# Hash attention and a gated MLP: a third Strassen product of the gated layer computed by halves, with its weight factors made in the first chunk

## The chip, the cores and the metric

The kernel runs on one core of a Trainium2 chip. The metric is device time in microseconds (us); the kernel before took 866.93 us (median of 3 runs, 865.80 to 868.44). TensorE (PE in the profile) multiplies, VectorE (DVE) and ScalarE (ACT) work on tiles, GpSimd (POOL) and SyncE (SP) mostly issue DMAs here. PEld is TensorE's loading of weights, which the profile lists beside the matmuls.

## The reference

```python
# attention: B=4, H=8, S=768, D=64; proj is [64, 6]
q_bits = (einsum('bhsd,dk->bhsk', q, proj) > 0)        # k_bits alike
mask   = q_bucket[:, :, :, None] == k_bucket[:, :, None, :]   # the 6 bits as a number
attn   = softmax(where(mask, q @ k.T / sqrt(D), -1e9))
x = (attn @ v).transpose(0, 2, 1, 3).reshape(3072, 512)
# the MLP: w_in [512, 2048], w_out [2048, 512]
r = maximum(x @ w_in, 0)
return (r * r) @ w_out                                   # float32, [3072, 512]
```

## The kernel before, in words

**Stages.** The attention comes first (0 to 317 us of the span; L341 to L812). It leaves x, transposed, in DRAM. The MLP then goes over the tokens in three chunks of 1024: a *gated layer* (x times w_in, then relu squared) followed by `project` (times w_out). The order of all work is written out by hand, so on every engine and every DMA queue the instructions run in the order of the program. A DMA that GpSimd, SyncE or ScalarE issues waits in that engine's own queue.

**The gated layer.** A chunk's h is 2048 x 1024: sixteen blocks of 128 rows, taken as eight *units* r, each of two row blocks (r and r + 8) times two halves of 512 tokens. Each unit is one level of Strassen-Winograd: seven products in place of eight, named by their token-side factor: "11", "21", "t1", "t2", "t3", "t4", "22". A product has two matmuls (f = 0, 1) of 128x128 weights and 512 columns. The weight-side factors of all units lie in DRAM as `w_in_7`; `load_unit` (L641) brings one unit's to SBUF on SyncE's queue. Sums go to banks acc0, acc1, acc2 of PSUM; partial sums that are used more than once are copied out by ScalarE: `one`, `two`, `three`, `five` (L842 in chunk 0, L1062 later; two buffers each). VectorE adds the copies to banks, and gates: h·max(h, 0), one instruction (L919). The gated results are b11, b12, b21, b22, from which sums for the next layer are made at once (b_t, b12 in the loop at L1338 and below; `inner_sums` L1099).

**Chunks 1 and 2 of the gated layer** go by four *pairs* of units, n and n + 4 (`hidden_pair` L1046). Of two of the seven products ("21" and "t4") both units' work is put together as one product of 512 columns and four row blocks, and this is done by a second level of Strassen-Winograd: seven matmuls of 256 columns in place of eight (that is, of four of 512). That is `inner_steps` (L995): four steps of two, two, two and one matmul, and `put` (L1039), which adds the inner result to the outer sums and gates it. Its matmuls are at L1007; its partial sums are copied into quarters of two `o` tiles (`snaps`). The first inner product runs in a pair's first half, the second in its second half, step by step between the outer products (L1054). The inner weight factors are sums over both units' weights. `factor_units` (L956) makes them for pair n during chunk 0's projection, in its products k = 1 to 4: GpSimd loads two `h` tiles of `w_in_7`, VectorE sums, GpSimd stores to `w_in_49` (L969). `load_inner` (L971) brings them back, on SyncE's queue, one pair ahead; for a chunk's first pair at product k = 6 of the chunk before. The token-side factors are `sums_inner` (L985), made in the hook of k = 6.

**`project`** (L1176) is one level over seven outer products k, each of which is again `product` (L826), by 256 columns. Each takes leaf tiles of w_out (128 x 512), asked for on ScalarE's queue (L1121). Its sums go to `sum0` to `sum3`, `tmp` and `o` (L1131), and out.

**Other things beside.** A guard decides whether a second, general program has to run: `load_peak` (L868) has GpSimd load q and k in 32 pieces of 128 x 2 x 384 (`raw_qk`, two buffers), and `peak` (L874) reduces each to its largest magnitudes, two in every unit of chunks 1 and 2, on VectorE, at the end of the unit. The guard's test is not met by this input in either kernel. In chunk 0 the factors of w_out are made too (`sums_out`, L1291, and `sums_out_49`, in units 0 to 5); after unit 5 their pool `p_1` is closed, and the pool `p_y` with leaf, sum, t, o and tmp tiles is opened. The x of the next chunk (2 MB) is asked for on GpSimd's queue at k = 0 of `project` (L633).

Of the kernel before, what the change touches and what calls it, by code (L numbers as in the profile page):

```python
# [27 lines left out]
PLAIN = 30.0  # L28
# [6 lines left out]
def kernel(  # L35
# [49 lines left out]
    w_in_49 = p_d.tile([NQ, P, 2, 7, P], FP32, name="w_in_49")  # L85
# [556 lines left out]
    def load_unit(n, pool=p_i):  # L642

        if n < NCHUNK * NR and n not in w_unit:
            r = order(n)
            w_unit[n] = pool.tile([P, 7, NFT // 2, P], FP32, name="w_unit", bufs=2 if pool is p_i else 1)
            m = 7 if n < NR else 5
            nc.sync.dma_start(out=w_unit[n][:, 0:m], in_=w_in_7[r, :, 0:m])
# [8 lines left out]
    with tc.manual_schedule():  # L657
# [167 lines left out]

        def product(n, w, at, bt, c11, c12, c21, c22, hook=None):  # L826

            acc = [ps_m.tile([P, 512], FP32, name=f"acc{i}")[:, 0:w] for i in range(3)]

            def add(to, a, b, first, last):
                for i in range(n):
                    nc.tensor.matmul(  # L835
                        out=acc[to], lhsT=a(i), rhs=b(i), start=first and i == 0,
                        stop=last and i == n - 1, skip_group_check=True,
                    )

            def keep(of, name):  # L840
                t = p_r.tile([P, 512], FP32, name=name)[:, 0:w]
                nc.scalar.copy(out=t, in_=acc[of])  # L842
                return t

            add(0, at(0), bt["11"], True, False)
            one = keep(0, "one")
            add(1, at(1), bt["21"], True, True)
            if hook:
                hook()
            c11(acc[1], one)  # L850
            add(0, at(4), bt["t2"], False, False)
            two = keep(0, "two")
            add(2, at(3), bt["t1"], True, False)
            five = keep(2, "five")
            add(0, at(5), bt["t3"], False, False)
            three = keep(0, "three")
            add(2, at(6), bt["22"], False, True)
            c12(acc[2], two)
            c22(three, five)
            add(0, at(2), bt["t4"], False, True)  # L860
            c21(acc[0])
# [12 lines left out]
        def peak(i):  # L874

            nc.vector.tensor_reduce(  # L876
                out=peaks[:, :, i], in_=raw_qk.pop(i), axis=AXL.X, op=ALU.max,
                apply_absolute_value=True,
            )
# [9 lines left out]
        def guard():  # L889

            most = p_k.tile([1, 2], FP32, name="most")
            tp = spare("tp")[:, 0]
            for w in range(2):
                nc.tensor.transpose(
                    out=tp[0:1, w * P:(w + 1) * P], in_=top[:, w:w + 1], identity=ident
                )
            nc.vector.tensor_reduce(
                out=most, in_=tp[0:1, 0:2 * P].rearrange("o (w f) -> o w f", w=2), axis=AXL.X,
                op=ALU.max,
            )  # L900
            nc.vector.tensor_scalar(
                out=slow, in0=most[:, 0:1], scalar1=most[:, 1:2], scalar2=PLAIN / (scale * D),
                op0=ALU.mult, op1=ALU.is_gt,
            )
# [26 lines left out]
        def hidden(i, r):  # L931
# [4 lines left out]
            def gate(out):  # L936
# [11 lines left out]
                gate(b22),  # L948
# [5 lines left out]
        w_inner, t_inner, snaps, now = {}, {}, {}, {}  # L954

        def factor_units(n):  # L956
# [9 lines left out]
            for lo, hi, t in (  # L966
                (0, 2, src[0]), (2, 3, src[1][:, :, 1:2]), (3, 5, sums[0]), (5, 7, sums[1])
            ):
                nc.gpsimd.dma_start(out=w_in_49[n, :, :, lo:hi], in_=t)  # L969

        def load_inner(i, n):  # L971

            if n < NQ:
                w_inner[i, n] = []
                for j, name in enumerate((("sum0", "sum3"), ("sum2", "sum1"))[n % 2]):
                    t = p_y.tile([P, 4, QN], FP32, name=name).rearrange("p a (b c) -> p (a b) c", c=P)
                    nc.sync.dma_start(out=t[:, 0:7], in_=w_in_49[n, :, j])
                    w_inner[i, n].append(t)

        def quarters_x(i, j):  # L980

            b = xs[i][0][:, 2:4, 0:HN] if j == 0 else xs[i][0][:, 0:2, HN:NCH]
            return b[:, 0, 0:QN], b[:, 0, QN:HN], b[:, 1, 0:QN], b[:, 1, QN:HN]

        def sums_inner(i):  # L985

            t_inner[i] = [p_y.tile([P, NQ, QN], FP32, name=f"t{m}", bufs=2) for m in range(2)]
# [7 lines left out]
        def inner_steps(i, n, j):  # L995
# [5 lines left out]
            if i not in snaps:  # L1001
                o = [p_y.tile([P, HN], FP32, name="o", bufs=NOUT) for _ in range(2)]
                snaps[i] = [o[m // 2][:, m % 2 * QN:(m % 2 + 1) * QN] for m in range(4)]
            one, two, three, five = snaps[i]

            def mul(out, a, b, start, stop):
                nc.tensor.matmul(  # L1007
                    out=out, lhsT=w[:, a], rhs=b, start=start, stop=stop, skip_group_check=True
                )

            def step_0():
                a0, a1 = (ps_m.tile([P, 512], FP32, name="acc1")[:, 0:QN] for _ in range(2))
# [7 lines left out]
            def step_1():  # L1020
                hs["a2"] = spare("acc3")[:, 0, 0:QN]
# [24 lines left out]
        def hidden_pair(i, n, half):  # L1046

            r = half * NQ + n
            w, bt = w_unit.pop(i * NR + 2 * n + half), factors_x(i)
            acc = {m: ps_m.tile([P, 512], FP32, name=f"acc{m}") for m in (0, 2)}  # L1050

            def add(to, a, b, first, last):
                for f in range(NFT // 2):
                    nc.tensor.matmul(  # L1054
                        out=acc[to], lhsT=w[:, PLACE[a], f], rhs=bt[b](f),
# [4 lines left out]
            def keep(of, name):  # L1060
                t = p_r.tile([P, 512], FP32, name=name)
                nc.scalar.copy(out=t, in_=acc[of])  # L1062
                return t

            if half == 0:
                load_inner(i, n + 1)
                now[0], now[1] = (inner_steps(i, n, j) for j in range(2))
            *steps, put = now[half]
            add(0, 0, "11", True, False)
            one = keep(0, "one")  # L1070
            if half:
                now[0][4](1, b11[:, r], one)
            else:
                steps[0]()
            add(2, 3, "t1", True, False)
            five = keep(2, "five")
            steps[1 - half]()
            add(0, 4, "t2", False, False)
            two = keep(0, "two")
            steps[2 - half]()  # L1080
            if half == 0:
                put(0, b11[:, r], one)
            add(2, 6, "22", False, True)
            gate_sum(b12[:, r], acc[2], two)
            steps[3 - half]()
            if half:
                put(0, b21[:, n], now["three"])
            add(0, 5, "t3", False, True)
            three = keep(0, "three")
            gate_sum(b22[:, r], three, five)  # L1090
            if half:
                steps[3]()
                put(1, b21[:, r], three)
            now["three"] = three
# [82 lines left out]
        def project(i):  # L1177
# [60 lines left out]
            for k in range(7):  # L1238
# [6 lines left out]
                if k == 6 and more:  # L1245
                    load_inner(i + 1, 0)
# [8 lines left out]
                def hook():  # L1255
# [4 lines left out]
                    if k == 6 and more:  # L1260
                        sums_inner(i + 1)
# [73 lines left out]
        for i in range(NCHUNK):  # L1335
            for s in range(NR):
                r = order(i * NR + s)
                if i == 0:  # L1338
                    hidden(i, r)
                else:  # L1340
                    hidden_pair(i, s // 2, s % 2)
                minus(b_t[:, r], b12[:, r], b11[:, r])
# [7 lines left out]
                if i == 0 and r == THEN[-1]:  # L1350
                    p_1s.close()
                    p_y = fast.enter_context(tc.tile_pool(name="p_y", bufs=1, reuse_waits="tile"))
                load_unit(i * NR + s + (3 if i == 0 and s < 2 else 2))
# [5 lines left out]
                if i > 0 and s % 2:  # L1359
                    inner_sums(0, slice(s // 2, s // 2 + 1))  # L1360
                minus(b12[:, r], b22[:, r], b12[:, r])
                for n in range(2):
                    m = 2 * ((i - 1) * NR + s) + n
                    if m >= 0:
                        peak(m)
# [241 lines left out]
```

## Time and profile before

| | us |
|---|---|
| median of 3 runs | 866.93 |
| the profiled execution, own time | 866.47 |
| its span, first to last instruction | 864.2 |
| mean granted clock of TensorE | 0.998 of full |

Stages of the span, from the busy times of each engine in the stretches (the bounds are rounded; DMA is the mean busy share of the 16 DMA engines):

| stage | us | PE busy | PEld | DVE | ACT | POOL | DMA |
|---|---|---|---|---|---|---|---|
| attention | 0–317 | 314.3 | 149.8 | 292.3 | 240.8 | 67.5 | 0.81 |
| chunk 0, gated layer | 317–413 | 96.0 | 42.6 | 82.5 | 24.2 | 35.6 | 0.85 |
| chunk 0, project | 413–499 | 84.8 | 74.0 | 77.5 | 11.8 | 21.5 | 0.85 |
| chunk 1, gated layer | 499–592 | 93.0 | 51.8 | 74.7 | 30.4 | 14.9 | 0.52 |
| chunk 1, project | 592–677 | 85.0 | 74.6 | 76.7 | 12.0 | 8.0 | 0.71 |
| chunk 2, gated layer | 677–770 | 93.0 | 51.8 | 73.7 | 30.8 | 14.9 | 0.48 |
| chunk 2, project | 770–855 | 84.9 | 74.0 | 69.9 | 11.6 | 5.2 | 0.59 |
| last output | 855–864 | 0.8 | 0.4 | 1.4 | 0.4 | 1.3 | 0.34 |

A row is read like this: in chunk 1's gated layer TensorE is busy all of the 93 us, VectorE 80% of them, and the transfers half. In the lists of groups a line such as `PE MATMUL acc<-t_x,w_unit 128*128 128x512 f32 x192` names engine, operation, the tile written, the tiles read, the weights' and the output's shapes, and the count. What follows in brackets is idle time and the instruction that ended it. A float32 matmul leaves two records. In the timeline, the first number is the start and the second the duration, in us.

### The profile page before, as it was taken

Reading aid. Unit: us, or ns where it says so; the run is one execution under the profiler, and the core shown is the slowest. Engines: PE = TensorE matmul, PEld = TensorE weight load, DVE = VectorE, ACT = ScalarE, POOL = GpSimd, SP = SyncE. Lnnn points to the kernel's source line nnn. Section 1 sums busy time; section 2 is a strip of 40 time slices with the busy share of each in tenths; the row PEclk is TensorE's granted clock in tenths of the full one; section 3 lists DMA queues with packets and bytes.
Section 4 is the critical chain, followed back from the end, with each engine's and each line's share of the span. In section 5 each row is a group of like instructions: output and inputs, shape, how many; then the busy total and the mean of one; then the engine's idle time right before and its main releaser. Section 6 shows DMA issues by size and latency. Waiting matters only on the chain.

```text
span 864.2 us, 16743 instructions
## 1 busy us (share of the span) xinstructions
PE 851.8 (99%) x6548; PEld 519.2 (60%) x6548; DVE 748.8 (87%) x1005; ACT 362.0 (42%) x648; POOL 168.9 (20%) x284
## 2 busy tenths in 40 slices
PE   8999999999999999999999999999999999999996
PEld 3544444444444444444888855557888655568885
DVE  5899999999999898988879978888799688888875
ACT  5887777888777752222111133332111233321110
POOL 1321111123221102642132211112001111100002
PEclk9999999999999999999999999999999999999999
DMA  9677799879997618999888864547757645355565
GB/s 206 129 152 148 178 182 205 203 166 257 244 229 192 200 53 276 317 322 284 292 269 258 177 168 157 176 120 263 246 156 191 161 157 175 118 162 159 147 185 98
DMA packets 226629, 168.03 MB, mean 194 GB/s; under 512 B 167112, under 2 KB 184848, under 8 KB 226544
## 3 DMA queue, kind: packets, MB, share of 16 engines
q1 hardware_dynamic: 187744, 87.19, 40.7%
q0 software_dynamic: 16416, 41.95, 15.7%
q10 hardware_dynamic: 22384, 37.76, 14.6%
q8 instruction: 53, 0.87, 0.4%
q14 instruction: 32, 0.26, 0.1%
HBM read 124.52 MB, written 41.68 MB: 192 GB/s over the span
## 4 chain that ended last, share of the span: by engine, by line
PE 98%; DVE 1%; issue 0%; POOL 0%; ACT 0%; POOLq 0%; DVEq 0%
PE acc L835 40%; PE st L430 18%; PE acc L1054 16%; PE xo L485 14%; PE acc L1007 6%; PE tot L534 2%; PE hash L360 1%; PE xo L337 1%; PE tp L320 0%; DVE bits L410 0%; DVE o L1131 0%; POOL out_dram L1152 0%; PE xo L360 0%; ACT e L436 0%; DVE tmp L1131 0%
## 5 line engine op out<-in xcount | busy, mean ns | idle before, releaser
L436 ACT ACTIVATE e<-st 128x768 f32<-128x768 f32 x192 | 155.3, 809 | 58.6 <-PE st L430 55.5
L430 PE MATMUL st<-feat 64*64 64x384 f32 x1536 | 157.4, 483 | 1.0 <-DVE feat L329 1.0
L485 PE MATMUL xo<-e,v_nat 64*64 64x385 f32 (+1 forms) x1520 | 157.1, 483 | 0.0
L835 PE MATMUL acc<-b,leaf 128*128 128x256 f32 x600 | 133.2, 379 | 1.2 <-issue 1.2
L835 PEld LDWEIGHTS acc<-b,leaf 128*128 128x128 f32 x600 | 113.8, 190 | 17.7 <-issue 2.3
L473 DVE TENSOR_TENSOR total<-total,e 128x1536 f32<-128x1536 f32 x64 | 111.7, 1746 | 4.3 <-ACT e L436 2.8
L396 POOL DMA_DIRECT2D bits<-signed x120 | 61.9, 520 | 218.2 <-ACT signed L385 199.6
L485 PEld LDWEIGHTS xo<-e,v_nat 64*64 64x64 f32 (+1 forms) x1520 | 56.3, 133 | 67.5 <-issue 59.3
L1054 PE MATMUL acc<-t_x,w_unit 128*128 128x512 f32 x192 | 90.2, 592 | 0.0
L430 PEld LDWEIGHTS st<-feat 64*64 64x64 f32 x1536 | 55.9, 133 | 39.3 <-issue 33.9
L835 PE MATMUL acc<-t,leaf 128*128 128x256 f32 x336 | 76.2, 380 | 0.0
L835 PEld LDWEIGHTS acc<-t,leaf 128*128 128x128 f32 x336 | 63.7, 190 | 9.1 <-DVE t L593 0.5
L919 DVE SCALAR_TENSOR_TENSOR b<-h 128x512 f32<-128x512 f32 x96 | 65.7, 691 | 3.0
L430 PE MATMUL st<-bits 64*64 64x384 bf16 x768 | 65.0, 325 | 0.1
L1054 PE MATMUL acc<-x,w_unit 128*128 128x512 f32 x128 | 60.2, 592 | 0.0
L835 PE MATMUL acc<-x,w_unit 128*128 128x512 f32 x128 | 56.5, 593 | 0.0
L1054 PEld LDWEIGHTS acc<-t_x,w_unit 128*128 128x128 f32 x192 | 36.5, 190 | 28.9 <-issue 26.8
L835 PE MATMUL acc<-b_t,leaf 128*128 128x256 f32 x240 | 53.8, 379 | 0.0
L1152 POOL DMA_DIRECT2D out_dram<-h x26 | 16.8, 654 | 174.1 <-DVE h L1145 167.0
L842 ACT COPY two<-acc 128x256 f32<-128x256 f32 (+1 forms) x29 | 12.5, 431 | 87.8 <-PE acc L835 75.3
L835 PEld LDWEIGHTS acc<-b_t,leaf 128*128 128x128 f32 x240 | 45.5, 190 | 6.2
L872 POOL DMA_DIRECT2D raw_qk<-in_q_dram x32 | 17.3, 541 | 162.4 <-DVE peaks L876 162.4
(155 smaller groups left out, 1194.2 us busy)
## 6 DMA issues: line engine op xcount, KB each, us to landing
leaf<-w_out ACTq DMA_DIRECT2D x142, 256.0 KB, 3.1
w_unit<-w_in SPq DMA_DIRECT2D x16, 640.0 KB, 4.0
raw<-in_moe_w_in_dram SPq DMA_DIRECT2D x8, 1024.0 KB, 6.3
raw<-in_moe_w_out_dram SPq DMA_DIRECT2D x8, 1024.0 KB, 7.4
w_unit<-w_in SPq DMA_DIRECT2D x8, 896.0 KB, 9.2
w_out<-sums POOLq DMA_DIRECT2D x16, 448.0 KB, 8.0
sum<-w_in SPq DMA_DIRECT2D x16, 448.0 KB, 4.9
v_nat<-in_v_dram SPq DMA_DIRECT2D x16, 384.0 KB, 5.1
```

The lines of the kernel that those rows point to most:

```text
L396: nc.gpsimd.dma_start(out=t[h * D:h * D + NBITS + 1, w, c * HS:(c + 1) * HS], in_=signed[at:at + NBITS + 1, h],)
L430: nc.tensor.matmul(out=st[k * HK:(k + 1) * HK, h, 0:HS], lhsT=src[1][rows, key], rhs=src[0][rows, cut], start=first, stop=not first, skip_ ...
L436: nc.scalar.activation(out=key_of(pr, kt)[:, :, i, 0:HS], in_=st[:, :, 0:HS], func=ACTF.Exp, scale=scale)
L473: nc.vector.tensor_tensor(out=totals[pr], in0=totals[pr], in1=e, op=ALU.add)
L485: return nc.tensor.matmul(out=outs[pr][h * D:(h + 1) * D, c, 0:HS + 1], lhsT=nat[pr, "v_nat"][rows, h, kt * D:(kt + 1) * D], rhs=key_of(pr ...
L534: done = nc.tensor.matmul(out=spares[pr][g * 32:(g + 1) * 32, c2, 0:QS], lhsT=ones[rows], rhs=totals[pr][rows, h, c, c2 * QS:(c2 + 1) * QS ...
L835: nc.tensor.matmul(out=acc[to], lhsT=a(i), rhs=b(i), start=first and i == 0, stop=last and i == n - 1, skip_group_check=True,)
L872: nc.gpsimd.dma_start(out=raw_qk[i][:, w], in_=flat[:, i * n:(i + 1) * n])
L919: nc.vector.scalar_tensor_tensor(out=out, in0=h, scalar=0.0, in1=h, op0=ALU.max, op1=ALU.mult)
L1007: nc.tensor.matmul(out=out, lhsT=w[:, a], rhs=b, start=start, stop=stop, skip_group_check=True)
L1054: nc.tensor.matmul(out=acc[to], lhsT=w[:, PLACE[a], f], rhs=bt[b](f), start=first and f == 0, stop=last and f == NFT // 2 - 1, skip_group_ ...
L1152: queue.dma_start(out=out[at, m0 + a * 32:m0 + (a + 1) * 32].rearrange("(c i) j -> i c j", i=32), in_=ot[a * 32:(a + 1) * 32].rearrange("i ...
```

## The change

Three things change, and some orders with them.

- **A third product by halves.** In chunks 1 and 2 the product "22" of both units of a pair also becomes an inner product of seven 256-column matmuls. The three are now called A ("21"), B ("22") and C ("t4"). `hidden_pair` is put in a new order: A's steps and B's first two in the first half, B's last two and C's in the second. "22" no longer shares acc2 with "t1"; instead VectorE adds `five` to `two` (tiles of 128x512), and B's `put` adds that sum to the inner result for b12. As the sums of b_t, b12 and of the next layer need b12 of both units, they move into the second half.
- **Its weight factors** are not made in `factor_units`, but for all four pairs at once in chunk 0: after unit 5, GpSimd loads the "22" weights of all units (two loads of 512 KB, into `sum0` and `sum1`); VectorE sums them in the hook of the last unit (four instructions), and GpSimd stores them (four DMAs) as a third plane of `w_in_49`. They come back in two leaf tiles a pair (`load_third_inner`), on SyncE's queue at the pair's first half for the next pair, and for a chunk's first pair on ScalarE's queue in the hook of k = 6. `load_unit` brings four factors in place of five (512 KB for 640). `sums_inner` makes a third set of four sums.
- **The first inner weights** of a chunk are asked for in two parts, at k = 5 and at k = 6, where both were asked for at k = 6.
- **The peaks** become squares with a running sum on ScalarE, four in a unit of 384 elements each, spread over the half; the guard's limit is squared to match.
- **Buffers.** `two` and `five` have one buffer in place of two, while `one` and `three` keep two. Inner copies use two sets, which alternate.

The diff, cut to its core:

```diff
-    w_in_49 = p_d.tile([NQ, P, 2, 7, P], FP32, name="w_in_49")
+    w_in_49 = p_d.tile([NQ, P, 3, 7, P], FP32, name="w_in_49")
...
-            m = 7 if n < NR else 5
+            m = 7 if n < NR else 4
...
+        KEPT = dict(one=2, two=1, three=2, five=1)
...
-                t = p_r.tile([P, 512], FP32, name=name)[:, 0:w]
+                t = p_r.tile([P, 512], FP32, name=name, bufs=KEPT[name])[:, 0:w]
...
-            nc.vector.tensor_reduce(
-                out=peaks[:, :, i], in_=raw_qk.pop(i), axis=AXL.X, op=ALU.max,
-                apply_absolute_value=True,
+            t = raw_qk[i][:, w]
+            nc.scalar.activation(
+                out=t, in_=t, func=ACTF.Square, accum_out=peaks[:, w, i:i + 1]
             )
...
+        def load_thirds():
+            for j in range(2):
+                thirds[j] = p_y.tile([P, 4, QN], FP32, name=f"sum{j}").rearrange(
+                    "p n (f c) -> p n f c", c=P
+                )
+                nc.gpsimd.dma_start(
+                    out=thirds[j],
+                    in_=w_in_7[j * NQ:(j + 1) * NQ, :, PLACE[6]].rearrange("n p f c -> p n f c"),
+                )
+        def sum_thirds():
...
+            sums_a(
+                *(thirds[j][:, :, f] for j in range(2) for f in range(2)),
+                *(sums[m // 2][:, :, m % 2] for m in range(4)),
+            )
+            for lo, hi, t in (
+                (0, 2, thirds[0]), (2, 3, thirds[1][:, :, 1:2]), (3, 5, sums[0]), (5, 7, sums[1])
+            ):
+                nc.gpsimd.dma_start(
+                    out=w_in_49[:, :, 2, lo:hi].rearrange("n p m c -> p n m c"), in_=t
+                )
...
+        def load_third_inner(i, n, queue):
+            if n < NQ:
+                ts = [p_y.tile([P, NQ, P], FP32, name="leaf", bufs=NLEAF) for _ in range(2)]
+                for m, t in enumerate(ts):
+                    hi = min(4 * m + 4, 7)
+                    queue.dma_start(out=t[:, 0:hi - 4 * m], in_=w_in_49[n, :, 2, 4 * m:hi])
+                w_inner[i, n].append(lambda a: ts[a // 4][:, a % 4])
...
-                snaps[i] = [o[m // 2][:, m % 2 * QN:(m % 2 + 1) * QN] for m in range(4)]
-            one, two, three, five = snaps[i]
+                o = [o[m // 2][:, m % 2 * QN:(m % 2 + 1) * QN] for m in range(3)]
+                snaps[i] = o, [t_inner[i][m][:, 3] for m in range(3)], spare("acc3")
+            side = (3 * n + (0, 2, 1)[j]) % 2
+            one, two, five = snaps[i][side]
+            three = one
+            last = snaps[i][2][:, side, 0:QN]
...
-                a0, a1 = (ps_m.tile([P, 512], FP32, name="acc1")[:, 0:QN] for _ in range(2))
+                a0, a1 = (ps_m.tile([P, 512], FP32, name=f"acc{m}")[:, 0:QN] for m in (1, 2))
...
+            A, B, C = (now[c] for c in "ABC")
+            add(acc, 0, "11", True, False)
+            one = keep(acc, "one")
             if half == 0:
+                A[0]()
             else:
+                B[2]()
+                C[0]()
+                A[4](1, b11[:, r], one)
+                B[4](0, b12[:, r0], now["two"])
+            mark()
+            other = ps_m.tile([P, 512], FP32, name="acc2")
+            add(other, 3, "t1", True, True)
+            five = keep(other, "five")
             if half == 0:
+                A[1]()
+            else:
+                B[3]()
+                C[1]()
+                minus(b_t[:, r0], b12[:, r0], b11[:, r0])
+                minus(b12[:, r0], b22[:, r0], b12[:, r0])
+            mark()
             add(acc, 4, "t2", False, False)
+            two = keep(acc, "two")
             if half == 0:
+                A[2]()
+                B[0]()
+                A[4](0, b11[:, r], one)
+                nc.vector.tensor_tensor(out=two, in0=two, in1=five, op=ALU.add)
+            else:
+                C[2]()
+                nc.vector.tensor_tensor(out=two, in0=two, in1=five, op=ALU.add)
+                B[4](1, b12[:, r], two)
+                minus(b_t[:, r], b12[:, r], b11[:, r])
+                inner_sums(0, slice(n, n + 1))
+                C[4](0, b21[:, r0], now["three"])
+            mark()
             add(acc, 5, "t3", False, True)
+            three = keep(acc, "three")
             if half == 0:
+                A[3]()
+                B[1]()
+                gate_sum(b22[:, r], three, five)
             else:
+                C[3]()
+                gate_sum(b22[:, r], three, five)
+                minus(b12[:, r], b22[:, r], b12[:, r])
+                C[4](1, b21[:, r], three)
+            mark()
...
-                if k == 6 and more:
-                    load_inner(i + 1, 0)
+                if k >= 5 and more:
+                    load_inner(i + 1, 0, (k - 5,))
...
+                        load_third_inner(i + 1, 0, nc.scalar)
...
-                    hidden(i, r)
+                    hidden(i, r, sum_thirds if s == NR - 1 else None)
...
+                    load_thirds()
...
-                    if m >= 0:
-                        peak(m)
```

## The prediction

> **What bounds the kernel now.** I read the summary first, then the chain of work that ended last, then who waited for whom on TensorE, then the timeline of one pair of units engine by engine.
>
> ```profile
> PE 851.8 (99%) x6548; PEld 519.2 (60%) x6548; DVE 748.8 (87%) x1005; ACT 362.0 (42%) x648; POOL 168.9 (20%) x284
> ...
> PE 98%; DVE 1%; issue 0%; POOL 0%; ACT 0%; POOLq 0%; DVEq 0%
> ```
>
> TensorE (PE) is the bound: 98% of the chain is its own work. On TensorE's list of waits all four together are 4.5 us, none of them in a pair. So a matmul column removed is time removed, as long as no new wait opens. The price of a matmul is the distance of groups in the chain (start, length, records; a float32 matmul is two records):
>
> ```profile
> 499.52 1.72 PE acc L1054 x4
> 501.24 0.86 PE acc L1007 x4
> 502.10 1.72 PE acc L1054 x4
> ```
>
> Two matmuls of 512 columns take 1.72 us, so 0.859 each; two of 256 take 0.86, so 0.430 each, with no loss for alternating. A pair now is 2x10x0.859 + 14x0.430 = 23.2 us; the chain has pairs starting at 522.73 and 545.94, 23.2 apart.
>
> **TensorE work removed.** Each pair trades four 512-column matmuls ("22", two f in two units) for seven of 256: 4x0.859 - 7x0.430 = 0.43 us. Four pairs in each of two chunks: 8x0.43 = **3.44 us** less. The pair becomes 16x0.859 + 21x0.430 = 22.8 us: first half 4 products (6.87) and eleven 256s (4.73), 11.6; second half 6.87 and ten 256s, 11.2.
>
> **A new short gap.** In the second half the copy `two` of acc0 must end before product "t3" adds to acc0, and only C's third step, two 256-column matmuls or 0.86 us, lies between. Before, at least 1.72 us lay there. Three rows of before price it; the first two are one pair's step and copy, the third a load that waited:
>
> ```profile
> 529.45 1.03 PE L1007 MATMUL acc<-x,sum 128*128 128x256 f32 x4
> ```
>
> ```profile
> 529.64 0.58 ACT L1062 COPY two<-acc 128x512 f32<-128x512 f32 x1 [1.34 <-PE acc L1054]
> ```
>
> ```profile
> 855.76 0.53 PEld L1162 LDWEIGHTS acc<-ident,o 128*128 128x128 f32 x4 [1.23 <-DVE o L1131]
> ```
>
> The copy starts 0.20 after the next group's first matmul and lasts 0.585 (group mean). That VectorE `o` started at 855.63 and took 0.41, so a waiting weight load starts 0.05 after its releaser: here at 0.84. The load itself waits, it doesn't go ahead. The first matmul of the first unit also began with its load not yet done: its record is 0.697 against 0.592, so an uncovered load costs 0.105. Thus "t3" starts at 0.84 + 0.105 = 0.945 where 0.859 was free: 0.086 us a pair, 8x = **0.69 us**. Bounds: nothing, if the load may go ahead (0.84 is under 0.859); 0.84 + 0.19 (whole load) - 0.859 = 0.17, or 1.37 in all. I take the row of a load that waited. TensorE's page of the Trainium skill ("TensorE: Matmul & The Clock Gate", section "Architectural detail: the array is 16× 32×32, not 1× 128×128") says that the queue can pull weight loads ahead of running matmuls; by it the term would be nothing, rival 1. The trace's only clear case, at 855.76, has the load waiting with its matmul.
>
> **VectorE (DVE).** Removed: 32 peaks of 0.945, four a pair. Added per pair: three 256-column adds of the new inner product (0.42 each) and two sums two+five (0.69 each). The total falls by 1.1 us a pair; what matters is the order, because the second half now holds most of it. The timeline's spacing is 0.60 for a 512-column instruction, 0.72 if the next needs its result; 0.34 and 0.45 at 256. Second half, TensorE's start as 0: C's third step is through at 9.03, seen by VectorE at 9.23. Behind it stand two adds 0.68, two+five 0.72, the b12 gate 1.44, b_t 0.60, three inner sums 1.13, the b21 gate 1.32, the b22 gate 1.44, b12 0.60, the last b21 gate 1.32: 9.25. VectorE ends at 18.5, TensorE at 11.2: **7.3 us late**. Before it was as late, through the peaks: the next half began at 522.57, and
>
> ```profile
> 528.14 1.81 DVE L876 TENSOR_REDUCE peaks<-raw_qk 128x2 f32<-128x768 f32 x2
> 529.87 0.41 DVE L1017 TENSOR_TENSOR h<-acc,o 128x256 f32<-128x256 f32 x1
> ```
>
> What is queued behind: the next pair's first add frees an acc2 bank at 7.3 + 0.41 + 0.05 = 7.76. B's first step wants that bank at 1.72+0.86+1.72+0.86+1.72+0.86+0.43 = 8.17, less 0.105 for the load: 8.06. Covered by 0.3; I take nothing. It decides from a lag of 7.6 on (rival 2). The single `five` buffer is freed by the b22 gate at 15.2 - 11.2 + 0.7 = 4.7 where its copy could start at 4.5; the copies then have 1 us of cover.
>
> **ScalarE (ACT).** Gains five copies of about 0.375 and eight squares a pair. A 384-element square with a running sum isn't in the trace; nearest, the 32x384 sign at L371 is 0.571 and the 384-element copy at L327 0.478; above, the 770-element copy 0.797. I take 0.57; the ends differ by 0.3, and ScalarE works some 14.9 of 22.8 us. The square ahead of the critical `two` can end 1.3 us before that copy is due, so both ends cost nothing. "ScalarE: Activation LUTs" in the Trainium skill (section "What ACT_TABLE_LOAD costs") gives 186 ns + 0.833 per element, an estimated 0.51; the sum would be the same. A square also waits for its raw_qk: GpSimd asks once the tile is read, two issues of 0.54 and 3.3 to landing, 4.4 in all where about 8 us lie between.
>
> **First chunk.** GpSimd's queue gets two loads of 512 KB and four stores, ahead of the peak loads, x and the `h` loads. The loads take the place of four raw_qk issued at 398.0 to 400.2, landing 6 us later; I put them at 406. VectorE's four sums (2.5) then end at 408.5, the gate behind (1.3) at 409.8; VectorE stood idle 5.01 us there until 411.81. Nothing lost. At the slowest GpSimd load's 12.5 us they land at 411.7: the first outer product's sums come 3.8 late, cover 1.4, so 2.4 us lost. The x load waits for TensorE until 414.23 anyway, and the first `h` land at 428.2 to 429.4 for a use at 432.85.
>
> The 1.25 us gap at 460 in the chain, called issue, ends when VectorE's b<-b,t (459.98, 1.22) does; VectorE had waited 5.20 us for an `h` load at 443.45. The change leaves that order: I keep it, bounds -1.25 to +1.25.
>
> **Other moves.** sums_inner is four adds longer (1.6 us): at the second entry VectorE freed the last acc2 at 676.1, then 677.7, wanted at 679.6. Asking for inner weights a product sooner, the smaller unit loads (512 for 640 KB) and 448 KB more per pair: no matmul waited for a DMA, and DMA share is 0.48 to 0.52 there; nothing, either way.
>
> **Sum.** The profiled execution took 866.47 us (span 864.2 and 2.3 around it): 866.47 - 3.44 + 0.69 = **863.7**. It is 0.46 under the median of the runs shown; from 866.93 it would be 864.2. About 0.3%, 2.6 us, is what a measurement of this kernel can tell from no change, and the forecast (-0.32%) lies just past it.
>
> **Rivals.**
> 1. The weight load goes ahead, no gap at "t3": 866.47 - 3.44 = 863.0. For: 0.84 against 0.859. Against: 855.76.
> 2. Slower: VectorE's backlog at the pair's seam holds the acc2 bank. Place: B's first step of the six pairs that follow a pair; price six times what the lag is over 7.6. If VectorE's 17 instructions took their full record and 0.05 each (9.66 + 0.85 for 9.25), the lag is 8.56 and the loss 5.8: 869.5. For: a cover of only 0.3. Against: before's spacing is shorter than its records, and the same lag is measured.
> 3. The thirds land late, or the gap at 460 grows: +1.3 to +2.4, about 865.5. For: the DMA engines are full from 380 to 405 (0.82 to 1.01 by windows). Against: the idle 5.01.
>
> **How the numbers follow.** Forecast 0.53, of which 0.39 past the bound and 0.14 short of it; rival 1 0.16; rival 2 0.15, of which 0.12 over 869 and 0.03 between; rival 3 0.16, of which 0.01 slower. Faster 0.39 + 0.16 = 0.55; slower 0.13; within 0.32. The forecast's own range is 862.9 to 864.8. With the lower end of the gap at 460 and rival 3, the range is 862.2 to 867.0: rival 2 and a little on either side are left out.
>
> **What would show it.** TensorE's records 48 more, busy near 848.4; pairs 22.8 to 22.9 apart. `two` ends 0.79 after C's third step begins, and "t3" begins 0.95 after it (0.86: rival 1). The first add of a pair starts 7.3 after the pair (over 7.6, with B's second matmul late: rival 2). Square near 0.57. The first chunk's sums start by 407, the first outer product unbroken. A wait on ScalarE for raw_qk, or on TensorE for VectorE in a pair, would make the forecast wrong.

## The result, and the profile after

The changed kernel takes **864.43 us** (median of 18 runs, 863.23 to 866.64); the kernel before took 866.76 (median of 18 runs, 865.54 to 869.26). The ratio is 0.9973, with a 95% interval of 0.9964 to 0.9982: 2.3 us less, 0.27%. The forecast from the median was 864.2; the profiled execution took 863.55 us (span 861.4) where 863.7 was forecast.

The page of the changed kernel (busy time, share of the span, instructions), and from it the engines' shares of the chain that ended last:

```profile
PE 849.1 (99%) x6596; PEld 529.3 (61%) x6596; DVE 748.9 (87%) x1025; ACT 408.2 (47%) x816; POOL 174.1 (20%) x290
...
PE 95%; DMA 2%; DVE 1%; issue 0%; POOL 0%; ACT 0%; ACTq 0%; POOLq 0%; DVEq 0%
```

TensorE has the 48 records more that were forecast, and is busy 2.7 us less (849.1 against 851.8; forecast was 848.4). VectorE's total stays as it was; ScalarE has 46 us more. New is DMA in the chain, 2%. That is the time that transfers took, and not the time that TensorE waited for them: two pieces, 11.2 us together, lie in the attention, where nothing was changed, and the third is one leaf tile, 9.9 us, in chunk 0's projection.

Where the 2.8 us between the two spans lie, from the starts of the stages in the two chains:

| stage | before, us | after, us | difference |
|---|---|---|---|
| attention, to the first unit | 317.09 | 317.25 | +0.16 |
| chunk 0, gated layer and project | 182.43 | 182.80 | +0.37 |
| chunk 1, gated layer | 92.84 | 91.50 | -1.34 |
| chunk 1, project | 84.75 | 84.61 | -0.14 |
| chunk 2, gated layer | 92.84 | 91.51 | -1.33 |
| chunk 2, project, output | 94.25 | 93.73 | -0.52 |

The eight pairs bring 2.67 us; forecast were 2.75. Nothing was changed in the attention, and over all profiles of this study it lasted 316.8 to 318.4 us. Two single executions can differ by that much without any change there, so spans are compared by stages below, and times by medians.

**The pair.** The end of one pair and the start of the next in the changed kernel's chain (start, length):

```profile
518.12 1.72 PE acc L1104 x4
519.83 0.86 PE acc L1057 x4
520.70 1.79 PE acc L1104 x4
...
522.92 1.72 PE acc L1104 x4
```

L1104 are the outer products, L1057 the inner steps. "t2" and C's third step have their plain lengths; "t3" has 1.79 in place of 1.72. The chain has pairs starting at 500.05 and 522.92, so 22.87 apart. Two timelines show what the group waits for, ScalarE's and that of the weight loads:

```profile
519.87 0.58 ACT L1112 COPY two<-acc 128x512 f32<-128x512 f32 x1 [0.83 <-PE acc L1104]
```

```profile
520.50 0.30 PEld L1104 LDWEIGHTS acc<-t_x,w_unit 128*128 128x128 f32 x2 [0.21 <-ACT two L1112]
```

The copy ends at 520.45 and the load begins 0.05 later, 0.83 after the first matmul record of C's step, at 519.67 (the chain, which goes by the work before it, has 519.83): both as forecast (0.84). What is lost is 0.08, not 0.086.

**VectorE at the seam.** The new pair starts at 522.92 and its first add at 530.02, 7.1 us late (forecast 7.3); the instruction before it is the last gate of the old pair:

```profile
529.42 0.69 DVE L921 SCALAR_TENSOR_TENSOR b<-h 128x512 f32<-128x512 f32 x1
530.02 0.42 DVE L1067 TENSOR_TENSOR h<-acc,t 128x256 f32<-128x256 f32 x1
```

**Chunk 0's projection** is where forecast and run differ. From TensorE's list of waits, and then its weight loads, in the changed kernel:

```profile
PE acc L837 <- ACT three L844: 0.5, 1, 0.5
PE acc L837 <- DMA leaf<-w_out: 0.2, 1, 0.2
```

```profile
422.64 1.59 PEld L837 LDWEIGHTS acc<-b,leaf 128*128 128x128 f32 x8 [0.83 <-ACT three L844]
424.57 1.59 PEld L837 LDWEIGHTS acc<-b,leaf 128*128 128x128 f32 x8 [0.34 <-issue]
426.63 1.59 PEld L837 LDWEIGHTS acc<-b,leaf 128*128 128x128 f32 x8 [0.48 <-DMA leaf<-w_out]
428.82 1.59 PEld L837 LDWEIGHTS acc<-b,leaf 128*128 128x128 f32 x8 [0.59 <-DMA leaf<-w_out]
430.71 1.38 PEld L837 LDWEIGHTS acc<-t,leaf 128*128 128x128 f32 x7 [0.30 <-issue]
```

Each product of four matmuls takes one new leaf tile, and five in a row come late. Three of the brackets name ScalarE's copy or "issue", but all five loads begin 0.04 to 0.11 us after their tile has landed (422.53, 424.46, 426.59, 428.77 and 430.60 by the trace). From 405 to 435 us a leaf tile takes 8.9 us to land (median), before it took 4.8. TensorE's waits for them come to 1.88 us, worked out as the sum of what the starts of neighbouring matmul records are apart beyond the usual 0.215. By the same sum the stop at 460 was 1.49 us before; it is gone. The two explain the stage: 1.88 - 1.49 = 0.39, where the table has +0.37.

What GpSimd asks for there is in another order. Before, and then in the changed kernel:

```profile
397.98 0.58 POOL L872 DMA_DIRECT2D raw_qk<-in_q_dram  x1
...
414.23 0.77 POOL L633 DMA_DIRECT2D x<-x_all  x1 [14.06 <-PE acc L835]
```

```profile
398.14 1.54 POOL L981 DMA_DIRECT2D sum<-w_in  x2
...
411.37 0.55 POOL L874 DMA_DIRECT2D raw_qk<-in_q_dram  x1
...
413.93 0.75 POOL L633 DMA_DIRECT2D x<-x_all  x1 [0.40 <-PE acc L837]
```

### The profile page after: what moved, and what is told of

It reads as the page before. It is cut to its first block, busy times and chain, and to the rows that moved or that the text cites. A ratio compares the mean times of both kernels' runs of the same rounds, so it can differ in the third digit from the quotient of the medians.

```text
span 861.4 us, 16973 instructions
## 1 busy us (share of the span) xinstructions
PE 849.1 (99%) x6596; PEld 529.3 (61%) x6596; DVE 748.9 (87%) x1025; ACT 408.2 (47%) x816; POOL 174.1 (20%) x290
## 4 chain that ended last, share of the span: by engine, by line
PE 95%; DMA 2%; DVE 1%; issue 0%; POOL 0%; ACT 0%; ACTq 0%; POOLq 0%; DVEq 0%
PE acc L837 40%; PE st L430 18%; PE xo L485 14%; PE acc L1104 13%; PE acc L1057 8%; PE tot L534 2%; PE hash L360 1%; DMA leaf<-w_out 1%; DMA bits<-signed 1%; DMA qk_nat<-in_k_dram 1%; POOL bits L396 0%; DVE bits L410 0%; PE xo L360 0%; DVE o L1210 0%; ACT e L436 0%
## 5 line engine op out<-in xcount | busy, mean ns | idle before, releaser
L1104 PE MATMUL acc<-t_x,w_unit 128*128 128x512 f32 x192 | 90.9, 595 | 0.0
L837 PE MATMUL acc<-x,w_unit 128*128 128x512 f32 x128 | 56.5, 593 | 0.0
L1104 PEld LDWEIGHTS acc<-t_x,w_unit 128*128 128x128 f32 x192 | 35.8, 190 | 26.7 <-issue 23.0
L844 ACT COPY one<-acc 128x256 f32<-128x256 f32 (+1 forms) x29 | 12.5, 431 | 77.6 <-PE acc L837 53.3
```

The source lines that it names most:

```text
L837: nc.tensor.matmul(out=acc[to], lhsT=a(i), rhs=b(i), start=first and i == 0, stop=last and i == n - 1, skip_group_check=True,)
L1104: nc.tensor.matmul(out=to, lhsT=w[:, PLACE[a], f], rhs=bt[b](f), start=first and f == 0, stop=last and f == NFT // 2 - 1, skip_group_check ...
```

## The experiments

The question that the result leaves is not the pairs but chunk 0: a new delay of 1.88 us appeared, an old one of 1.49 went away, and the forecast had neither. The kernels below change the changed kernel, unless "before" is said. In the table "420-431" and "460" are TensorE's stops there, in us, from one profile of each; "rest" names others. The kernels were timed in several rounds, each beside the kernel before, whose median was 866.4 to 866.8; the ratio is to that round's kernel before.

| kernel | median, us | ratio to before, 95% | 420-431 | 460 | rest |
|---|---|---|---|---|---|
| before | 866.76 | | 0 | 1.49 | |
| the change | 864.43 | 0.9973 [0.9964, 0.9982] | 1.88 | 0 | t3 0.64 |
| e1_step_between | 863.40 | 0.9964 [0.9951, 0.9976] | 1.56 | 0 | |
| e2_qk_later | 862.44 | 0.9960 [0.9945, 0.9975] | 0.36 | 0 | t3 0.64; chunk 1 entry 0.40 |
| e3_sums_in_hook | 863.72 | 0.9966 [0.9953, 0.9979] | 2.38 | 0 | t3 0.64 |
| e4_qk_and_hook | 861.99 | 0.9948 [0.9935, 0.9960] | 1.08 | 0 | t3 0.64 |
| e5_before_hook | 865.88 | 0.9991 [0.9982, 1.0000] | 0 | 0 | |
| e6_no_thirds | 862.82 | 0.9954 [0.9940, 0.9968] | 0.89 | 0 | t3 0.64; chunk 1 entry 0.35 |
| e7_peaks_on_vector | 869.97 | 1.0040 [1.0026, 1.0054] | 1.00 | 0.49 | 6.0 in chunks 1 and 2, t3 0.64 |
| e8_inner_at_six | 864.64 | 0.9980 [0.9970, 0.9989] | 1.83 | 0 | t3 0.64; chunk 1 entry 0.96 |
| e9_before_squares | 866.12 | 0.9992 [0.9983, 1.0001] | 1.41 | 0 | chunk 1 entry 1.08 |
| e10_all | 861.39 | 0.9942 [0.9930, 0.9954] | 0.97 | 0 | |
| e11_step_and_qk | 861.61 | 0.9940 [0.9927, 0.9953] | 0 | 0.91 | |
| e12_all_x_later | 864.55 | 0.9981 [0.9971, 0.9991] | 0.11 | 2.7, then 1.7 at half clock | |

### e1_step_between: the short gap

```diff
             else:
-                B[3]()
                 C[1]()
...
                 C[2]()
+                B[3]()
                 nc.vector.tensor_tensor(out=two, in0=two, in1=five, op=ALU.add)
```

> Changed kernel, with one 256-column step more (B's last) between the products "t2" and "t3" of a pair's second half. Theory: a pair lasts 22.87 us in the changed kernel where its matmuls add up to 22.80, because the weight load of "t3" waits for the copy of "t2" and is then not covered; with 1.29 us of other matmuls between, the pair lasts 22.80 and the group of "t3" 1.72 in place of 1.79, 8 x 0.075 = 0.6 us less in all, about 863.8. Rival: the 0.07 has another cause in the pair (the alternation of 512 and 256 columns, or a bank), then pairs stay at 22.87 and the time at 864.4. The time alone can hardly tell 0.6 us; the distances of the pairs can.

The same stretch of the chain in this kernel:

```profile
517.71 1.72 PE acc L1104 x4
519.42 1.29 PE acc L1057 x6
520.72 1.72 PE acc L1104 x4
...
522.87 1.72 PE acc L1104 x4
```

With 1.29 of other matmuls ahead of it, "t3" has 1.72 again, in all eight pairs, and pairs are 22.80 apart (500.07, 522.87). The short gap is the cause; the rival falls. The median is 1.0 lower, more than the 0.64, but well inside the intervals.

### e2, e3, e4: two delays of chunk 0's projection

```diff
# e2: the first q and k pieces
-                    if 0 <= m + 2 < NPK:
+                    if 2 <= m + 2 < NPK:
                         load_peak(m + 2)
...
+                if i == 0 and k == 6:
+                    for m in range(2):
+                        load_peak(m)
# e3: the inner factors' sums, moved into the hook of product k
-                if i == 0 and 0 < k <= NQ:
-                    factor_units(k - 1)
...
                         inner_sums(k + 1)
+                    if i == 0 and 0 < k <= NQ:
+                        factor_units(k - 1)
# e4: both
```

> Changed kernel, with the first two q and k pieces (four loads of 192 KB, which the changed kernel asks for at 411 to 413 us) asked for at the last product of chunk 0's projection. Theory: TensorE stops five times between 421.8 and 431, some 1.8 us in all, as leaf tiles of the first outer product land 8 to 10 us after their issue, behind what the thirds pushed into 411 to 428; without these 0.77 MB, at about 400 GB/s 1.9 us of transfers, the stops shrink to under 0.5 us. TensorE is then no longer late when VectorE's sum at 460 is due, and the stop of about 1.2 us at 460 comes back; in all 864.0 to 864.4, no gain that can be measured. Rival: the stops come from the thirds' own stores or the 2 MB of x; then they stay at 1.5 to 1.9 us and the time at 864.4, without a stop at 460.

The stops of 420 to 431 shrink to 0.36, as the theory had it, but the stop at 460 does not come back, and the time is 2.0 lower where no gain was expected. So the half of the theory that tied the two delays to each other missed here: VectorE's wait for the `h` load ended at 441.95 in this profile, not at 443.45 as before, and its sum was in time. On the other hand TensorE now comes early to chunk 1, and there waits 0.40 for the acc2 bank that VectorE frees at 500.8.

> Changed kernel, with the sums for the inner factors (four 256-column VectorE instructions a product, and their loads and stores in the same order) put behind the sums of the next outer product instead of ahead of them. Theory: VectorE's sum that TensorE waited for at 460 in the kernel before is late because VectorE stands 3.6 to 5.2 us before these sums at 443; put behind, that wait shrinks and the sum ends 3 us or more sooner. In the changed kernel TensorE comes to that place 1.8 us later and doesn't wait there, so this alone brings 0 to 0.2 us: 864.2 to 864.4. Rival: the lateness of 460 matters still, then the time falls by over 1 us.

As expected: no stop at 460 to be gained, the stops of 420 to 431 as large as ever. The 0.7 of the median lies within the intervals.

> Both edits on the changed kernel: the first q and k pieces later, and the inner factors' sums behind the next outer product's. Theory: the two delays of chunk 0's projection hide each other (TensorE 1.8 us late through leaf tiles, or 1.2 to 1.4 us waiting for VectorE), so only both edits together gain: TensorE runs from 317 to the first pair with stops under 0.5 us, 1.3 to 1.8 us less than the changed kernel, about 862.8. Rival: the two add up without overlap, or the stops move on to another product; then no gain, 864.4.

2.4 less than the changed kernel, but only 0.45 less than e2 alone: "only both edits together gain" is wrong; asking for the q and k pieces later does nearly all of it. Three pairs of kernels differ in that edit alone, and all go the same way: the change and e2 -2.0, e3 and e4 -1.7, e1 and e11 -1.8 by the medians, -1.1, -1.6 and -2.1 by the ratios, since two of the pairs were timed in different rounds. The intervals of each pair overlap; it is the three together that show the gain.

The landing times say the same. Of the seven leaf tiles asked for from 413 to 424 us, the median lands after 8.7 to 10.2 us in the five kernels that ask for the q and k pieces just ahead (the change, e1, e3, e7, e8), and after 7.1 to 8.4 in the eight that don't (e12 apart, see below).

### e5_before_hook: what the stop at 460 was

The edit of e3, on the kernel before.

> Kernel before, with the sums for the inner factors put behind the sums of the next outer product (the edit of e3). Theory: TensorE's stop at 460 (spacing 1.63 where 0.21 is usual, so 1.41 us) is VectorE's b<-b,t, late because VectorE stood 5.2 us before the inner factors' sums at 443; with those sums behind, the stop is gone and the time falls by 1.0 to 1.4 us, from 866.4 to about 865.2. Rival: the stop, called issue by the profile, has another cause; then it stays and the time is 866.4.

VectorE's timelines, the kernel before and then this one: the sum for the product at 460 starts 2.6 us sooner.

```profile
459.98 1.22 DVE L593 TENSOR_TENSOR b<-b,t 128x1024 f32<-128x1024 f32 x1
```

```profile
457.41 1.22 DVE L593 TENSOR_TENSOR b<-b,t 128x1024 f32<-128x1024 f32 x1
```

The stop is gone in the profile, so it was VectorE's, which the page calls "issue". The time falls by 0.9, less than the 1.0 to 1.4 expected, and with an interval of 0 to 1.6 it is hardly told from no change.

### e6_no_thirds: chunk 0 without the new work

```diff
-                    load_thirds()
...
-                    hidden(i, r, sum_thirds if s == NR - 1 else None)
+                    hidden(i, r)
...
-                    queue.dma_start(out=t[:, 0:hi - 4 * m], in_=w_in_49[n, :, 2, 4 * m:hi])
+                    queue.dma_start(out=t[:, 0:hi - 4 * m], in_=w_in_49[n, :, 1, 4 * m:hi])
```

> Changed kernel, without the loads, sums and stores of the third factors in chunk 0; the third inner product reads the second's factors instead, so b12 is computed with other weights, and nothing else differs. Theory: the q and k pieces are asked for at 398 to 400 us again and land before x is asked for, so leaf tiles are not late and the five stops of 420 to 431 (1.8 us) are gone; chunk 0 with its projection takes 181.0 us where the h loads land early, as in e2, or 182.3 where the stop at 460 returns, against 182.7; the time is 862.2 to 864.2. Rival: the stops come from x and the leaf tiles alone, with a new place of p_y's tiles; then they stay at 1.5 us or more, and the time at 864.4.

Without the sums of the thirds this kernel's b12 is another one; only its time is read. It came out in the range, 1.6 below the changed kernel, but the stops did not vanish: 0.89. Here theory and rival each have a half.

### e9_before_squares: the kernel before, with squares

Its diff is the change's own `peak`, and a `mark()` after each of the four steps of a half.

> Kernel before, with the peaks as four squares with a running sum on ScalarE in each unit of chunks 1 and 2, one behind each quarter of a half. Theory: VectorE is not what TensorE waits for in the pairs of the kernel before, so taking 32 instructions of 0.945 from it changes nothing: pairs stay 23.2 us apart, 866.4 within 0.3. Rival: the gain of the change comes from VectorE's relief; then 1 us or more falls, below 865.4. A third way: the squares hold up ScalarE's copies; then pairs get longer and the time rises over 867.

866.12, no difference that can be told, and pairs as in the kernel before: VectorE's relief by itself brings nothing. Its profile shows more than was asked: its chunk 0 is that of the kernel before, without thirds, and still has leaf stops of 1.41 at 423 to 429, and then none at 460. So the thirds are not needed for late leaf tiles, and the two delays take each other's place within one program.

### e11 and e12: which transfer

e11 is e1 and e2 together; e12 is e1, e2 and e3, and x later:

```diff
-                if k == 0 and more:
-                    load_x(i + 1)
...
                     if i == 0 and 0 < k <= NQ:
                         factor_units(k - 1)
+                    if k == 1 and more:
+                        load_x(i + 1)
```

> Changed kernel with the step between t2 and t3 (e1) and the first q and k pieces later (e2), and the inner factors' sums where they were. Theory: as e2 less 0.64: 861.8, with the stop of 0.3 to 0.4 us at the first inner step of chunk 1 that e2 had (VectorE frees acc2 late), and stops under 0.7 us at 420 to 431. Rival: the stop at 460 comes back (1.4 us) because the h load lands later than in e2; then 862.8 to 863.2.

Its rival happened in the profile: no leaf stops at all, and a stop of 0.91 at 460, for VectorE waited 4.80 us for an `h` load:

```profile
443.43 0.43 DVE L587 TENSOR_TENSOR h<-h 128x256 f32<-128x256 f32 x1 [4.80 <-DMA h<-w_in]
...
459.97 1.22 DVE L593 TENSOR_TENSOR b<-b,t 128x1024 f32<-128x1024 f32 x1
```

The time is at the theory's 861.8 all the same.

> As e10, and the 2 MB of the next chunk's x are asked for behind the first inner factors' loads, sums and stores, at about 435 us instead of 414. Theory: what makes the leaf tiles of the first outer product late is x, h, and leaf tiles together at 380 to 415 GB/s from 413 to 428; without x the stops of 420 to 431 vanish (0.1 us or less, in e4 0.86), about 0.7 us less than e10. Rival: x then crowds the h loads and leaf tiles of 435 to 450, and stops of 0.5 us or more come up there: no gain over e10, or a loss.

The leaf stops vanish (0.11), and the seven leaf tiles of 413 to 424 land after 5.0 us (median; 8.1 in e10): x is what they collide with most. The stops of a single profile would not show that, for e11 has none either, with x in its old place. But the `h` loads, asked for behind x, are used 7 us later than in the change (443.65 there); GpSimd's and VectorE's timelines:

```profile
436.43 0.77 POOL L633 DMA_DIRECT2D x<-x_all  x1
437.19 1.10 POOL L964 DMA_DIRECT2D h<-w_in  x2
```

```profile
450.72 0.42 DVE L587 TENSOR_TENSOR h<-h 128x256 f32<-128x256 f32 x1 [4.92 <-DMA h<-w_in]
```

TensorE stops for 2.7 at 460, until VectorE's sum is done. Then its matmuls run at half speed: from 462.8 to 466.2 the granted clock is 0.50, and eight records are 0.43 apart in place of 0.215, which costs 1.7 more. The stretch of 464 to 466 (its length, the busy times of PE, PEld, DVE, ACT and POOL, then the clock):

```profile
464.00:466.00 2.00, 2.00 (x6) 1.62 (x5) 1.86 (x6) 0.00 (x0) 2.00 (x4) 0.50 0.47 162
```

In the other profiles the clock stays at 1.00 from 8 us of the span on until the last matmuls are over, also behind a stop of 1.4 us (before, at 460). e12 is 3.2 slower than e10, which differs in x alone. The rival was right in kind; it named loads and leaf tiles at 435 to 450, and it was VectorE behind them at 460.

### e7_peaks_on_vector: what the squares are for

```diff
             t = raw_qk[i][:, w]
-            nc.scalar.activation(
-                out=t, in_=t, func=ACTF.Square, accum_out=peaks[:, w, i:i + 1]
...
+                    if m >= 0:
+                        peak(m)
```

(`peak` is that of the kernel before again.)

> Changed kernel, with the peaks on VectorE as in the kernel before (two of 0.945 us at the end of each half). Theory: VectorE comes to a new pair 7.1 us late in the changed kernel, and the acc2 bank of B's first step has cover up to 7.6; two peaks more make it 9.0, so TensorE stops about 1.4 us in each of the six pairs that follow a pair: 8 us, about 873, 870 to 876. Rival: the bank does not bind, or VectorE makes it up; then 864.4 to 865, and the squares on ScalarE were not needed.

5.5 us slower than the change, and 0.4% slower than the kernel before: the squares were needed. But the place was not the one named. In this kernel the second pair starts at 522.74; TensorE's timeline (L1057 with `leaf` weights at 530.31 is B's first step) and VectorE's:

```profile
530.31 1.03 PE L1057 MATMUL acc<-x,leaf 128*128 128x256 f32 x4
531.18 1.88 PE L1104 MATMUL acc<-t_x,w_unit 128*128 128x512 f32 x4
```

```profile
529.84 1.81 DVE L878 TENSOR_REDUCE peaks<-raw_qk 128x2 f32<-128x768 f32 x2
531.56 0.41 DVE L1067 TENSOR_TENSOR h<-acc,t 128x256 f32<-128x256 f32 x1
```

VectorE is 8.8 us late, 1.2 past the alleged limit of 7.6, and B's first step runs without a stop: its second matmul, which needs the bank, begins at 530.74, 0.8 ahead of the add that was to free it. Of the two acc2 banks it must then have written the other one, which the copy `five` had left, and not the one that A's first add reads. The loss comes later: VectorE has 84.3 us of work in the 91.7 of chunk 1's pairs (73.2 of 91.5 in the change), so it enters the projection behind, and TensorE's stops lie there (2.24 in chunk 1's, 1.95 in chunk 2's) and in chunk 2's pairs (1.8 besides t3). Two of the three in chunk 1's, 1.8 together, end 0.06 to 0.07 after a sum of VectorE does.

### e8_inner_at_six: the first inner weights

```diff
-                if k >= 5 and more:
-                    load_inner(i + 1, 0, (k - 5,))
+                if k == 6 and more:
+                    load_inner(i + 1, 0)
```

> Changed kernel, with both inner weight tiles of a chunk's first pair asked for at k = 6, as before, in place of one at k = 5 and one at k = 6. Theory: at k = 5 the tile is issued at 484.7 and lands 5.3 us later, ten us early; at k = 6 SyncE comes to it after eight output transfers, at 496.2, so it lands at about 501.5 to 502.5, where TensorE wants it at 501.6; e9 stopped there for 0.97 us. So a stop of 0 to 1 us at the first inner step of chunk 1, less in chunk 2; 864.4 to 865.4. Rival, and my own costing: the part for k = 5 brings nothing; no stop, 864.4.

SyncE's timeline, first in the change, then in e8: at k = 5 one tile is asked for ahead of the second eight output transfers, at k = 6 both are behind.

```profile
484.74 0.34 SPq L1010 DMA_DIRECT2D sum<-w_in  x1
488.86 7.32 SPq L1231 DMA_DIRECT2D out_dram<-h  x8
496.23 0.51 SPq L1010 DMA_DIRECT2D sum<-w_in  x1
```

```profile
481.76 15.16 SPq L1231 DMA_DIRECT2D out_dram<-h  x11
497.16 0.87 SPq L1010 DMA_DIRECT2D sum<-w_in  x2
```

TensorE then stops for 0.96 at chunk 1's first inner step, and in e9, which asks at k = 6 too, for 1.08:

```profile
PE acc L1057 <- DMA sum<-w_in: 0.7, 1, 0.7
```

Chunk 2 shows none. By the medians (864.64 and 864.43) it can't be told.

### e10_all: the best version

e1, e2 and e3 together.

> Changed kernel with three edits: the step between t2 and t3 (e1), the first q and k pieces later (e2), the inner factors' sums behind the next outer product's (e3). Theory: the terms add: pairs 22.80 apart without the 0.08 of t3 (-0.64), chunk 0 with its projection at 181.2 to 182.0 as in e2 and e4 against 182.7; 861.4, 860.9 to 862.4. Rival: VectorE, which frees the bank for the first inner step of chunk 1 only 0.5 us before it is wanted in the changed kernel, takes the gain of chunk 0 back; then 862.4 to 863.

861.39, as the sum of the terms: 3.0 less than the change and 5.1 less than before, with an interval clear of the change's. e11, without e3's edit, can't be told from it (861.61); so e1 and e2 make this version, and e3's edit can be left out.

## Why the prediction was right

**Right, step by step.** The columns removed (3.44) less the gap at "t3" (0.69 forecast, 0.64 measured, and removed by e1) give the pairs' 2.75 against 2.67. Both terms are a little large: a pair is 22.80 in e1, without the gap, and 23.21 before, so the columns bring 3.3. The sum rounded 0.426 a pair up to 0.43, and a 256-column matmul takes 0.432 by the spacing of its records (0.2158 each) where it has 0.430. The copy, the load that waits for it and the load's cost came out to 0.01 us. One sign of the list reads otherwise, though: the first matmul record of "t3" begins 0.86 after C's step, which was named as the sign of rival 1. The wait does not move that record; it makes it longer (0.67 in place of 0.59). It is the load's start and e1 that decide against rival 1.

The Trainium skill ("TensorE: Matmul & The Clock Gate", section "Architectural detail: the array is 16× 32×32, not 1× 128×128") says that TensorE's queue can pull weight loads ahead of running matmuls; were it so for this load, the gap would cost nothing. The trace agrees for a load that waits for no other engine: the third of "t3" begins at 521.04, 0.43 ahead of its matmul record. The first begins 0.05 after the copy ends, so here one that waits was not pulled ahead, and the measurement decides.

The lag of VectorE at the seam is 7.1 (forecast 7.3). A square lasts 0.53, within the bounds, but leaves a second instruction of 0.20, reading the sum, that was not foreseen; ScalarE had room for both, as forecast. VectorE's total was to fall by some 3 us (1.1 less a pair, 2.5 and twice 1.6 more for the new sums) and did not; it cost nothing. ScalarE's groups in chunk 1's gated layer:

```profile
L879 ACT ACTIVATE raw_qk<-raw_qk 128x384 f32<-128x384 f32 x32 | 17.0, 533 | 0.0
L879 ACT ACTIVATION_READ_ACCUMULATOR raw_qk<-raw_qk 128x1 f32 x31 | 6.2, 199 | 0.0
```

**Wrong: "Nothing lost" in the first chunk.** The price was put on VectorE, and there it held (its sums started at 407.70, the forecast of the landing was 406). The step left out the q and k pieces: they were asked for 13 us later, at 411 to 413, straight ahead of x and the leaf tiles of the first outer product. TensorE lost 1.88 us to late leaf tiles, within rival 3's price (1.3 to 2.4) but through another mechanism; three comparisons give 1.7 to 2.0 for this order of loads by medians, 1.1 to 2.1 by ratios.

**Wrong: "I keep it" for the stop at 460.** It did not stay. TensorE comes to that place 1.88 later, and VectorE's sum is then in time. So the two errors nearly cancelled, +1.88 - 1.49, and that was luck. The forecast's closeness rests partly on it; the range held either way, since either error alone would have left the time inside it.

**Wrong: rival 2's place.** The acc2 bank does not bind at 7.6; e7 passed it by 1.2 without a stop. A VectorE with 3.8 us more per pair does make the kernel slower (+0.4%), by the total of its work, which goes into the projections, not by one bank. The chance given to a slower kernel rested on the wrong cover.

**Wrong: "Asking for inner weights a product sooner ... nothing".** It removes a stop of 1 us that the old order has in some executions (0.96 in e8, 1.08 in e9, none in the profile of before).

**Open.** Why the `h` load lands at 442 in one profile and at 443.45 in another, and so which of the two delays of chunk 0 a given execution shows; single profiles of kernels without the late q and k pieces have leaf stops from 0 to 1.41, those with them 1.00 to 2.38. The three comparisons and the landing times bear out the order of the loads; a share for each transfer can't be given. That the stop of 2.7 us brought on e12's half clock is not shown; one profile has both. The 0.52 less in the last stage was not looked into: about 0.16 of it are short stops of before that the change does not show.

## What to carry to other kernels

Count the work removed on the bound engine, then list every transfer whose place in its queue moves, also those that the change doesn't speak of, and see which stage they land in: here the late asking for four loads of 192 KB cost 1.1 to 2.1 us, where the arithmetic gained 2.67. Two delays in a row on one chain need not add: if the second engine is late by about as much, removing one can show the other, so test both edits together and apart. When an accumulator is copied before the next product adds to it, put at least the copy and a weight load, here 0.94 us (the 0.86 that lay there and the 0.08 lost), of other matmuls between (tested were 0.86 and 1.29); reordering one step did it for nothing.

## What was not expected of the hardware

A square with a running sum on ScalarE is two instructions, 0.53 and 0.20 us for 128x384. A leaf tile of 256 KB, asked for from 413 to 424 us, took 7.1 to 8.4 us to land (medians of seven in eight kernels) with x asked for at about the same time, 8.7 to 10.2 with the pieces of q and k just ahead as well, and 5.0 with x asked for later (e12). Behind a stop of TensorE of 2.7 us its granted clock was 0.50 for 3.4 us, once (e12).
